# Loads, weighing and the last block of a two-layer spectral mixer: tables and odd weight copies on GpSimd's queue, one product per unit, two PSUM banks at the ends

## The chip, the cores and the metric

The kernel runs on one core of a Trainium2 chip. The metric is the device time of one execution in microseconds (us). PE is TensorE, ACT ScalarE, DVE VectorE, POOL GpSimd, SP SyncE; SP and ACT and POOL each have a queue that issues DMA transfers.

## The reference, cut to what matters

Two kinds of layers alternate, A, B, A, B, on a state x of 2048 rows by 512 columns (bf16):

```python
def _A_ref(x, w_r, w_i):          # spectral
    X = rfft2(x); X = X * (w_r + 1j * w_i)
    return irfft2(X)
def _B_ref(x, w1, w2, w3, w4):    # mixer and MLP
    h = gelu(layernorm(x) @ w1)
    # quarters of h's columns shifted by -1, +1, -2, +2 rows, then joined
    hs = concatenate([g0, g1, g2, g3]) @ w2
    x1 = x + hs
    return x1 + gelu(layernorm(x1) @ w3) @ w4
x = x + _A_ref(layernorm(x), w_r, w_i)
x = x + _B_ref(layernorm(x), ...)
x = x + _A_ref(layernorm(x), w_r, w_i)
x = x + _B_ref(layernorm(x), ...)
```

w1 and w2 are 512x512, w3 is 512x1792, w4 is 1792x512; w_r and w_i are 2048x257. Both A layers use the same weights, and so do both B layers.

## The kernel before

The state stays in SBUF as 128 partitions by 16 "rows" q of 512 columns. The code calls one A and one B together a layer, layer A in the first pass and layer B in the second (`ORDER_A`, `ORDER_B`). The Fourier transforms are products with tables: T over the partitions, FA over the columns, TL over the 16 rows q, and back through TR, G and Tinv.

A layer runs in these steps; the letter is the name of the step in the written orders.

- Norm and first product (`O`, `over_p`): the norm's factor of a row is multiplied into a copy of the table T (`Q`, `scaled_T`), PE multiplies, and the result is taken from PSUM into V (`G`, `take_V`). All 16 rows must be in V before the next step.
- `d`, `t`: product with FA for a unit of one or two blocks b of frequencies (`UNITS`: blocks 0, 1, 14, 15 are single, the rest pairs), taken into TV.
- `q`, `x`: product with TL, taken into X.
- `p` (`weigh`): X times the weights W, one product with each of the two planes, into PB.
- `b`, `m`: product with TR, taken into hT (`take_b`). Block 15 is the last; its take is divided between ACT and DVE ("B" in `TAKE_B`).
- `D`, `Y`, `P`, `a`: back over the columns and the partitions, added to x. `D` needs all 16 blocks.
- `s`, `r`, `n`, `T`, `v`, `h`, `u`, `f`: norm, DMA transpose, w1, Gelu, w2 and residual.
- `R`, `o`, `U`, `w`, `g`, `W`, `A`: norm, DMA transpose, w3, Gelu, w4 and residual. In the first pass the next layer's norm (`B`, `j`, `S`, `Q`), first products (`O`) and takes (`G`) follow between them; in the second, the stores (`y`).

TL holds two halves. The second is the first with neighbouring columns exchanged and one sign changed, made by GpSimd (`turn_TL`, L216). W is loaded for 64 of 128 partitions in 4 groups of 8 (`load_W`, L202, four copies of each group, two of them in reverse order of rows); GpSimd's queue then copies each group to the other 64 partitions (L213, called double 0 to double 3 here). Two negations (`N0`, `N1`, L710) make a third plane of TR.

What each engine does in what order is written out by hand in `ORDER_0` (the first norm), `ORDER_A` and `ORDER_B`. A step names its number, for a copy the engine (V for DVE, else ACT), and after a point the PSUM bank. `X` steps are products of zeros that keep PE at work (`fill`, L241); `z` loads the Gelu table on ACT (`gelu_table`, L712). In the first norm, rows in `ON_ACT` get their sums from ACT (`mean`, `square`, and `from_means` on GpSimd), the others theirs from DVE (bn_stats, `s`; aggregate, `i`). `S` is the square root on ACT and `J` the reciprocal on DVE; both are done once for each group of `GROUPS`.

SP issues all loads in one sequence: x, FA, half of TL, the groups of W with TR and the other half of TL between them, G and Tinv; later a small copy called gate, which reads W and so waits for double 3, and the four MLP weights behind it (`load_mlp`). The DMA transposes go through SP too. On GpSimd's queue:

```python
    for k, f in enumerate(K.later):
        if k < 2:
            turn_TL(K, slice(8 * k, 8 * k + 8))
        f()
    K.load_mlp()
```

## Time and profile before

| | us |
|---|---|
| median of 3 runs | 354.09 (353.81 to 354.54) |
| profiled execution, its own time | 354.05 |
| its span, first to last instruction | 352.1 |
| first norm ends, first `d` starts at | 21.15 |
| first `D` of layer A starts at | 42.06 |
| first `v` of layer A starts at | 57.30 |
| first `d` of layer B starts at | 189.15 |
| first `D` of layer B starts at | 208.99 |
| last matmul ends about | 348.7 |

The profile is of one execution. Times in it count from the start of the span. In a line of a timeline the first number is the start, the second the length, then the engine, the line of the source and the operation, output and input, and how many instructions were merged; in brackets how long the engine was idle before, and what ended that. A group line has the busy time, the mean length in ns, and idle time. Matmuls overlap, so that their ends are modelled. A core's DMA share is the mean over its 16 DMA engines.

### The profile page before, as it was taken

The numbers are of one execution on the slowest core, as the hardware profiler recorded it, in microseconds if no ns is written. First come the engines' busy times: TensorE is split into PE (matmuls) and PEld (weight loads), VectorE is DVE, ScalarE is ACT, GpSimd is POOL, SyncE is SP. The second block draws the span as 40 slices with busy tenths as digits, with TensorE's granted clock in tenths as the row PEclk, the third lists the DMA queues.
The fourth block names the chain that finished last, engine by engine and source line by source line (L and its number), as shares of the span: only waits on it lengthen the run. The fifth ranks groups of instructions, "written<-read, shape, count | busy, mean of one in ns | idle before, by whom it ended". The sixth has DMA issues, their size and how long they took to land.

```text
span 352.1 us, 5565 instructions
## 1 busy us (share of the span) xinstructions
PE 338.8 (96%) x2103; PEld 188.2 (53%) x2124; DVE 184.5 (52%) x442; ACT 200.5 (57%) x355; POOL 68.2 (19%) x171
## 2 busy tenths in 40 slices
PE   7889899999999999999999999999999999999996
PEld 5667785444444444444557888544444444444442
DVE  4869989669270445176586988845732004001003
ACT  5989899585736406213416979976583660442400
POOL 1430037462030101001120003645050010000000
PEclk9999999999999999999999999999999999999999
DMA  7995926611030030300000000663003005101003
GB/s 245 267 335 197 383 88 120 119 32 30 1 61 0 0 61 13 76 0 2 1 2 0 2 2 2 121 106 64 11 7 85 0 0 106 45 0 47 0 30 104
DMA packets 47210, 24.35 MB, mean 69 GB/s; under 512 B 36816, under 2 KB 43984, under 8 KB 47184
## 3 DMA queue, kind: packets, MB, share of 16 engines
q1 hardware_dynamic: 46464, 21.84, 24.7%
q0 software_dynamic: 576, 2.11, 1.5%
q8 instruction: 16, 0.26, 0.3%
q14 instruction: 10, 0.08, 0.1%
q10 hardware_dynamic: 144, 0.07, 0.1%
HBM read 11.41 MB, written 2.10 MB: 38 GB/s over the span
## 4 chain that ended last, share of the span: by engine, by line
PE 77%; ACT 8%; DMA 6%; DVE 4%; issue 3%; SPq 1%; POOL 1%; DVEq 0%; POOLq 0%; ACTq 0%
PE ps L655 26%; PE ps L642 26%; PE ps L591 8%; PE ps L607 8%; ACT hT L151 2%; PE ps L540 2%; PE ps L552 2%; DMA xT<-xn 2%; DMA W<-W 2%; PE ps L476 1%; DMA x_state<-in_A_x_dram 1%; ACT gT L649 1%; DVE PB L515 1%; ACT X L151 1%; DMA W<-in_A_w_i_dram 1%
## 5 line engine op out<-in xcount | busy, mean ns | idle before, releaser
L649 ACT ACTIVATE gT<-ps 128x1024 bf16<-128x1024 f32 x56 | 56.5, 1023 | 84.2 <-PE ps L642 81.1
L642 PE MATMUL ps<-xT,w 128*128 128x512 bf16 x448 | 99.3, 379 | 0.0
L655 PE MATMUL ps<-w,gT 128*128 128x512 bf16 x433 | 97.7, 379 | 0.8
L660 DVE TENSOR_TENSOR x_state<-ps,x_state 128x512 bf16<-128x512 f32 x32 | 21.5, 688 | 111.7 <-PE ps L655 111.7
L642 PEld LDWEIGHTS <-w 128*128 128x128 bf16 x448 | 43.8, 98 | 52.9
L655 PEld LDWEIGHTS <-gT 128*128 128x128 bf16 x448 | 43.7, 98 | 52.2
L615 DVE SCALAR_TENSOR_TENSOR xn<-xn,ln_c,ps 128x512 bf16<-128x512 bf16 x32 | 23.2, 744 | 18.5 <-PE ps L607 16.1
L270 ACT ACTIVATE junk<-xn 128x512 bf16<-128x512 bf16 x32 | 19.9, 624 | 16.8 <-DVE xn L615 16.8
L607 PE MATMUL ps<-w,hT 128*128 128x512 bf16 x122 | 28.8, 379 | 0.3
L591 PE MATMUL ps<-xT,w 128*128 128x512 bf16 x128 | 28.4, 379 | 0.5 <-DMA xT<-xn 0.5
L276 POOL TENSOR_SCALAR ln_mv<-ln_s 128x4 f32<-128x4 f32 x16 | 5.5, 344 | 91.1 <-DVE x_state L560 52.1
L560 DVE SCALAR_TENSOR_TENSOR x_state<-ps,x_state 128x512 bf16<-128x512 f32 x32 | 20.4, 684 | 2.6 <-PE ps L552 1.9
L515 DVE TENSOR_TENSOR PB<-X,W 128x1024 bf16<-128x1024 bf16 (+1 forms) x40 | 21.0, 580 | 0.1
L591 PEld LDWEIGHTS <-w 128*128 128x128 bf16 x128 | 12.3, 98 | 15.8 <-issue 1.2
L257 DVE BATCH_NORM_STATS2 ln_st<-x_state 128x6 f32<-128x512 bf16 x28 | 18.7, 686 | 3.8 <-DMA x_state<-in_A_x_dram 3.6
L607 PEld LDWEIGHTS <-hT 128*128 128x128 bf16 x128 | 12.5, 98 | 15.1
L270 ACT ACTIVATE xn<-x_state 128x512 bf16<-128x512 bf16 x32 | 19.7, 620 | 0.5 <-DVE x_state L560 0.2
L598 ACT ACTIVATE hT<-ps 128x512 bf16<-128x512 f32 x32 | 17.1, 599 | 1.4 <-PE ps L591 1.3
L540 PE MATMUL ps<-G,hT 128*128 128x256 bf16 x128 | 15.1, 273 | 2.1 <-DVE hT L149 1.2
L476 PE MATMUL ps<-FA,V 128*128 128x256 bf16 x128 | 16.1, 273 | 0.8 <-ACT V L151 0.8
L552 PE MATMUL ps<-Y,Tinv 128*128 128x256 bf16 x128 | 15.8, 272 | 0.7 <-DVE Y L149 0.5
L524 PE MATMUL ps<-TR,PB 128*128 128x128 bf16 x256 | 16.0, 219 | 0.0
(78 smaller groups left out, 387.0 us busy)
## 6 DMA issues: line engine op xcount, KB each, us to landing
w<-in_B_w_dram SPq DMA_DIRECT2D x2, 1792.0 KB, 11.9
W<-W POOLq DMA_DIRECT2D x4, 514.0 KB, 6.0
x_state<-in_A_x_dram SPq DMA_DIRECT2D x8, 256.0 KB, 5.7
out_dram<-x_state SPq DMA_DIRECT2D x16, 128.0 KB, 1.9
TR<-tab_TR SPq DMA_DIRECT2D x2, 512.0 KB, 5.8
w<-in_B_w_dram SPq DMA_DIRECT2D x2, 512.0 KB, 4.5
W<-in_A_w_r_dram SPq DMA_DIRECT2D x7, 128.5 KB, 5.7
W<-in_A_w_i_dram SPq DMA_DIRECT2D x7, 128.5 KB, 4.9
```

What stands on the lines that cost most here:

```text
L270: K.nc.scalar.activation(out, src, ACT.Square, bias=0.0, scale=D ** -0.5, accum_out=self.s[:, i, 1:2])
L515: nc.vector.tensor_tensor(t[:, :, 0:n], x, w, op=ALU.mult)
L540: nc.tensor.matmul(o[:, i, e * 256:(e + 1) * 256], lhsT=M[:, F, e, 2 * m + i, :], rhs=K.G[:, F, e, :], start=(F == 0 and e == 0), stop=(F ...
L552: nc.tensor.matmul(o[:, h * 256:(h + 1) * 256], lhsT=K.Tinv[:, c], rhs=rhs[:, ::-1] if h else rhs, start=(e == 0), stop=(e == 1))
L560: nc.vector.scalar_tensor_tensor(K.x[:, q, :], ps.pop(("P", q)), 1.0, K.x[:, q, :], op0=ALU.mult, op1=ALU.add, accum_out=ln[g].s[:, i, 0:1])
L591: nc.tensor.matmul(o[:, i], lhsT=K.w1[:, t, j * P:(j + 1) * P], rhs=xT[g][:, :, t, :], start=(t == 0), stop=(t == 3))
L607: nc.tensor.matmul(o, lhsT=K.hT[:, j, st:st + P], rhs=K.w2[:, j, :], start=(j == 0), stop=(j == 3))
L615: nc.vector.scalar_tensor_tensor(xn[:, q, :], xn[:, q, :], ln[q // 4].c[:, q % 4:q % 4 + 1], ps.pop(("u", n)), op0=ALU.mult, op1=ALU.add, ...
L642: nc.tensor.matmul(o[:, i], lhsT=K.w3[:, c, t * P:(t + 1) * P], rhs=xT3[g][:, :, c, :], start=(c == 0), stop=(c == 3))
L649: nc.scalar.activation(gT[g][:, 2 * j:2 * j + 2, :], ps.pop(("w", k)), ACT.Gelu_apprx_tanh, bias=0.0, scale=1.0)
L655: nc.tensor.matmul(o, lhsT=gT[g][:, t, i * P:(i + 1) * P], rhs=K.w4[:, t, :], start=(t == 0), stop=(t == 13))
L660: nc.vector.tensor_tensor(K.x[:, q, :], ps.pop(("W", n)), K.x[:, q, :], op=ALU.add)
```

## The change

SP loads x and then the groups of W. FA, TL and TR move to GpSimd's queue, as do the two copies of W's row 32; G and Tinv move behind the gate copy. TL's halves become contiguous. The two products of `weigh` become one of twice the size, with X read twice; PB and X get another layout for it, and the units in `LATE` share the large slots. Block 15 of the products `b`, row 15 of the first norm and row 15 of the later norm are put in two PSUM banks, one for each engine that takes them; row 15 of the first norm was taken by ACT alone before. In the first norm, two rows instead of four get their sums on ACT, groups are five instead of six, and the variance from sums is made row by row. All three orders are new; `z0` stands behind the first Gelus now, and the number of fills in the first norm falls from 16 to 12.

```diff
     for h in range(8):
         nc.sync.dma_start(K.x[:, h * 2:h * 2 + 2, :], xv[:, h * 2:h * 2 + 2, :])
-    table("FA", nc.sync)
-    K.TL = K.const.tile([P, NB, 2, P], BF16, name="TL")
+    K.W = K.const.tile([P, 2, NH, 257], BF16, name="W")
+    planes = [w.rearrange("(m j) f -> m j f", j=64) for w in (A_w_r, A_w_i)]
+    for pl, v in enumerate(planes):
+        nc.gpsimd.dma_start(K.W[2::4, pl, 0], v[:, 32])
+    for lo in range(0, NH, 8):
+        for pl, v in enumerate(planes):
+            load_W(K, v, pl, lo, lo + 8)
+    K.TL = K.const.tile([P, 2, NB, P], BF16, name="TL")
...
-        if lo == 8:
-            load_TL(slice(8, 16))
-        if lo in (0, 16):
-            nc.sync.dma_start(K.TR[:, 0:2, lo:lo + 16], dram["TR"][:, :, lo:lo + 16])
-    for k in ("G", "Tinv"):
-        table(k, nc.sync)
+
+    def load_rest():
+        q = nc.gpsimd
+        load_TL = lambda k: q.dma_start(K.TL[:, 0, 8 * k:8 * k + 8], dram["TL"][:, 8 * k:8 * k + 8])
+        load_TR = lambda k: q.dma_start(K.TR[:, 0:2, 16 * k:16 * k + 16], dram["TR"][:, :, 16 * k:16 * k + 16])
+        double = lambda k: q.dma_start(K.W[1::2, :, 8 * k:8 * k + 8], K.W[0::2, :, 8 * k:8 * k + 8])
+        table("FA", q)
+        load_TL(0)
+        load_TL(1)
+        load_TR(0)
+        double(0)
+        turn_TL(K, slice(0, 8))
+        double(1)
+        turn_TL(K, slice(8, 16))
+        double(2)
+        double(3)
+        load_TR(1)
...
         nc.sync.dma_start(gate2[:], K.W[1:2, 1, NH - 1, 1:17])
+        for k in ("G", "Tinv"):
+            table(k, nc.sync)
...
-    def from_means(self):
+    def from_means(self, i):
...
-def over_p(K, qs):
+def over_p(K, qs, split=False):
-    ps = banks(K, len(qs))
+    ps = banks(K, 2 if split else len(qs))
...
-            o = ps[:, i, t * 256:(t + 1) * 256]
+            o = ps[:, t, 0:256] if split else ps[:, i, t * 256:(t + 1) * 256]
...
     if part:
-        sl = slice(0, 64) if eng == "A" else slice(64, 128)
-    copy(K, dst[:, sl], src[:, sl], eng)
+        t = "AV".index(eng)
+        dst, ps = dst[:, 64 * t:64 * t + 64], ps[:, t:t + 1, 0:256]
+    copy(K, dst, ps.rearrange("d q (tb c) -> d tb q c", c=4), eng)
...
     def weigh(u):
         n = len(UNITS[u])
-        x = X.pop(u)[:, :, 0:256 * n].rearrange("p h (n f) -> p h n f", f=256)
-        pab[u] = []
-        for pl in range(2):
-            t = PB[n_pab[0] % 14 // 7][:, n_pab[0] % 7]
-            n_pab[0] += 1
-            w = K.W[:, pl, 2 * u:2 * u + 2 * n, 1:257].rearrange("p (n h) f -> p h n f", h=2)
-            nc.vector.tensor_tensor(t[:, :, 0:n], x, w, op=ALU.mult)
-            pab[u].append(t)
+        small = n == 1 and u not in LATE[last]
+        k = n_pab[small]
+        n_pab[small] += 1
+        if small:
+            t = PB[k % 2][:, 6].rearrange("p (l h) f -> p l h f", l=2)
+        else:
+            t = PB[k % 2][:, 2 * (k % 6 // 2):2 * (k % 6 // 2) + 2, 0:2 * n]
+        pab[u] = t
+        nc.vector.tensor_tensor(t, X.pop(u)[:, 0:2 * n].unsqueeze(1).to_broadcast([P, 2, 2 * n, 256]),
+                                K.W[:, :, 2 * u:2 * u + 2 * n, 1:257], op=ALU.mult)
...
-        ps["b", b] = o = banks(K, 1)[:, 0]
+        both = TAKE_B[last][b] == "B"
+        ps["b", b] = o = banks(K, 1 + both)
...
+        if TAKE_B[last][b] == "B":
+            F = "VA".index(eng)
+            dst, src = dst[:, :, 2 * F:2 * F + 2], ps["b", b][:, F, 0:256]
...
-FILL = {0: 4, 1: 3, 2: 3, 3: 3, 4: 3}
-GROUPS = [[0, 2, 3, 4], [7, 8, 9, 10], [11, 12], [14, 15], [1, 5], [6, 13]]
-ON_ACT = [1, 5, 6, 13]
-FIRST = [[0, 2], [3, 4], [1, 5], [7, 8], [9, 10], [11, 12], [6, 13], [14], [15]]
+FILL = {0: 3, 1: 3, 2: 2, 3: 2, 4: 2}
+GROUPS = [[0, 1, 2, 3], [4, 5, 6, 7], [8, 9, 10, 11], [12, 13], [14, 15]]
+ON_ACT = [1, 5]
+FIRST = [[0, 1], [2, 3], [4, 5], [6, 7], [8, 9], [10, 11], [12, 13], [14], [15]]
+LATE = ((14, 15), (0, 14))
 ORDER_0 = """
-s0 s2 s1 s3 i3 s5 f4 i0 i2 s4 i4 S0 s7 J0 Q0P s6 Q3V Q4V s8 s10 S4 J4 i7 O1 Q2A O0 s9 s13 Q1P i8 f5 i10 i9 Q5V s11 S1
-G1A J1 Q9V Q10V Q8P S5 s12 G0A i11 i12 O2 S2 O4 J5 Q7P s15 J2 G2A s14 i14 i15 Q12V Q11P O3 G4A Q6P S3 G3V O5 Q13A J3
-Q15V Q14P O6 G6V G5A O8 G8A O7 G7A
+s0 s2 i2 s3 i3 i0 s1 f0 s4 S0 J0 i4 Q1V Q0V s5 Q3V s6 s7 i6 i7 Q2A s11 s10 O0 G0A f1 S1 J1 s8 O1 G1A Q6A s9 Q7A i10
+i11 Q4A i9 i8 S2 s12 Q5A J2 Q10A O3 s13 G3A Q11V i13 i12 Q9V Q8V s14 S3 s15 i14 i15 O2 J3 Q12V G2A S4 J4 O5 G5A Q15A
+Q13V Q14V O4 G4V O6 G6A O7 G7V O8 G8V G8A
 """
 ORDER_A = """
...
-b14.0 m13A m11V b8.7 m8A m14V b15.5 m15A m15V D1.1 D0.5 z0 L13 Y1V Y0A D3.3 P2.0 a2 Y3A P3.7 a3 s2 P1.6 a1 P0.0 a0
...
-s13 s14 r2 P12.5 a12 L9 n8V v0.2 n11V n10V s12 r3 v1.0 h1 n9V T4 h0 v3.5 v2.0 h3 u0.7 h2 n12V n15V L14 T5 c0 u2.1 n14A
...
-S13 Q15 O15.7 A14 B14 j14 S14 Q13 O4.0 G4A G15V O6.3 G6A X4.0 Q14 O14.6 G14A X4.6 G4V G15A X8.2
...
+b13.1 m13V b8.3 m8A b14.4 m14A b15.5 m15A m15V D1.2 D0.4 D3.6 Y0A Y3A Y1V P2.1 a2 P3.4 P0.3 P1.0 s2 a3 s3 a0 s0 a1 s1
...
+n8V v0.6 v1.4 h0 c1 a14 T3 h1 T2 v3.0 s15 v2.6 s13 h3 u0.4 n10V T5 h2 u1.2 s12 f1 s14 u2.1 f2 k1 r3 c3 f0 E0 u3.7 n14V
...
+k6 w3.1 f14 E14 g3 z0 k13 L3 w1.5 g1 w4.0 g4 w0.3 g0 w2.1 g2 u9.5 f9 E6 k14 E9 E5 w6.3 E10 g6 w5.0 R1 g5 k8 E4 o4V o5V
...
+B14 O15.6 G15A S13 G4A j14 S14 Q13 O6.0 G15V G6A X4.4 Q14 O14.5 G14A X8.6 X4.5 G4V
 """
```

## The prediction

> **What bounds the kernel now.** I read the page first (busy line and chain of waits), then busy time by stage, then the timelines of single engines where a stage begins or ends. The page says that TensorE is nearly always at work:
>
> ```profile
> PE 338.8 (96%) x2103; PEld 188.2 (53%) x2124; DVE 184.5 (52%) x442; ACT 200.5 (57%) x355; POOL 68.2 (19%) x171
> ```
>
> That is an average. The stage table (stretch, length, then busy time of PE, PEld, DVE, ACT, POOL, granted clock, DMA share, GB/s) shows where it is not so:
>
> ```profile
> 3.90:21.15 17.25, 13.46 (x112) 10.75 (x110) 13.87 (x39) 15.43 (x38) 5.33 (x10) 1.00 0.96 292
> 21.15:42.06 20.91, 19.61 (x257) 15.90 (x257) 18.68 (x34) 19.13 (x27) 3.15 (x5) 1.00 0.81 298
> 42.06:57.30 15.24, 14.64 (x129) 12.43 (x130) 13.46 (x36) 14.06 (x31) 6.66 (x19) 1.00 0.53 139
> 57.30:186.00 128.70, 128.12 (x625) 60.53 (x636) 71.83 (x182) 59.24 (x102) 26.07 (x63) 1.00 0.16 30
> 189.15:208.99 19.84, 19.02 (x258) 15.95 (x256) 17.80 (x30) 17.45 (x27) 0.00 (x0) 1.00 0.01 2
> 224.00:348.70 124.70, 124.10 (x566) 56.16 (x576) 33.47 (x83) 59.10 (x101) 19.43 (x50) 1.00 0.20 42
> ```
>
> In the two long matmul stretches, 253 us, PE is busy 99.5%: nothing is won there, only lost. The change bears on the first norm (to 21.15) and on the two spectral middles (21.15 to 42.06, 189.15 to 208.99), where VectorE and ScalarE share one load at 85 to 93% each, so the sum of their work sets the length. The clock is 1.00 throughout.
>
> **Part 1, first norm.** The first product over all rows (d) starts at 21.15, when the last take of V has ended. I use the distance between starts in unbroken runs. ACT: a row's two sums 1.23 us, scaled table 0.40, pair take 0.90, square root 0.19. DVE: bn_stats 0.62, aggregate 0.09, reciprocal 0.12, scaled table 0.20, pair take 1.15. Before, ACT has 4×1.23 + 6×0.19 + 9×0.40 + 5×0.90 + 1.0 (two single takes) = 15.2; DVE 12×0.62 + 12×0.09 + 6×0.12 + 7×0.20 + 2×1.15 = 12.9. After, ACT has 2×1.23 + 5×0.19 + 7×0.40 + 6×0.90 + 0.3 (half a row) = 11.9; DVE 14×0.62 + 14×0.09 + 5×0.12 + 9×0.20 + 1.15 + 0.62 + 0.36 = 14.5. The busier engine falls by 0.7. Walking the new order by hand from the first x at 3.98, with x rows 4 and 5 at 6.46 as now, the last half take ends near 19.5: a gain of 1.65. I take 1.2, between the two.
>
> **Part 2, the loads.** SP issues x and then W alone: sixteen copies from 4.5 on by about 0.65 us end near 15, where FA, TL and TR between them made it 21.9 (two small W copies go first on GpSimd's queue, before any x has landed). FA, both halves of TL and TR now stand on GpSimd's queue behind the variances of rows 1 and 5, which it gets near 8.5. One issue there takes 0.61 to 0.87 us and landing took 6.0 to 6.6: FA at 16, needed at 19.9; TL's first half at 16.5, its turn (1.65 + 0.76) done by 19, needed by q near 21.3. Behind that turn wait double 1, the second turn, doubles 2 and 3 (which wait for W), then TR's second half. Now double 1 is held back by the second turn (GpSimd's timeline, then two pieces of the chain of waits):
>
> ```profile
> 20.18 1.65 POOL L219 TENSOR_SCALAR TL<-TL 128x512 bf16<-128x512 bf16 x1 [4.26 <-DMA TL<-tab_TL]
> 22.41 5.84 DMA W<-W
> 28.94 1.90 DVE PB L515 x3
> ```
>
> It lands at 28.25, just as DVE comes free for the products of units 2 and 4, so it costs at most 0.1. After, I expect it near 24. TR's second half, needed by its negation (N1) near 31, lands near 29. G and Tinv move behind the gate copy, which waits for double 3 (about 29); only the MLP weights stand behind them on SP; G lands near 34 and is needed near 39. I cost this part at nothing: FA is covered by 4 us, first turn and TR by about 2 each; without cover, each us late is a us lost.
>
> [...] The turn runs beside scaled tables on DVE:
>
> ```profile
> 12.79 1.66 POOL L219 TENSOR_SCALAR TL<-TL 128x512 bf16<-128x512 bf16 x1
> 12.90 0.78 DVE L348 TENSOR_SCALAR Tq<-T,ln_r 128x256 bf16<-128x256 bf16 x2
> 16.23 0.25 DVE L348 TENSOR_SCALAR Tq<-T,ln_r 128x256 bf16<-128x256 bf16 x1
> ```
>
> Two of them beside the turn took 0.78; two in a row elsewhere took 0.48: 0.3 lost. [...]
>
> **Part 3, weighing.** Two products per unit become one of twice the size:
>
> ```profile
> L515 DVE TENSOR_TENSOR PB<-X,W 128x1024 bf16<-128x1024 bf16 x24 | 15.2, 687 | 0.0
> L515 DVE TENSOR_TENSOR PB<-X,W 128x512 bf16<-128x512 bf16 x16 | 6.0, 420 | 0.1
> ```
>
> [...] One operation instead of two saves 0.07 to 0.08, ten times a layer: 0.74. The new operand reads X twice with a step of zero. No row shows that; nearest are these rows (0.53 per 1024 elements), the other end is half that rate: a pair 0.08 + 2.14 = 2.2 instead of 1.22, a single 1.15 instead of 0.69, 7.7 a layer. [...] Its free places stay as distant as now: the late units' slots are reused only after both halves of an earlier unit were multiplied. The orders also move work: in layer A one take of 128x512 (0.6) goes from ACT to DVE, so the sum of both engines falls by about 0.65, 0.3 each. In layer B the two end at about 16.6 and 17.8 against 17.8 and 17.5, so I take 0.1.
>
> **Part 4, last block in two banks.** ACT and DVE take block 15 one after the other now:
>
> ```profile
> 39.65 1.89 ACT L151 ACTIVATE hT<-ps 128x512 bf16<-128x512 f32 x4
> 41.58 0.43 DVE L149 CAST hT<-ps 128x256 bf16<-128x256 f32 x1 [0.58 <-ACT hT L151]
> 42.06 1.16 PE L540 MATMUL ps<-G,hT 128*128 128x256 bf16 x9 [1.24 <-DVE hT L149]
> ```
>
> PE stands behind both. Side by side it saves one half: 0.45 in A, 0.4 in B. The extra bank has to be free at its matmuls; it was left long before. With Part 3: 0.8 in A (0.35 + 0.45), 0.5 in B.
>
> **Part 5, turn of the layers.** DVE ends the last fold at 188.21, ACT its last take about 188.06, yet d starts at 189.15: twelve fills stand before it, four of which share the bank that ACT frees at 187.8.
>
> ```profile
> 186.23 1.83 ACT L151 ACTIVATE V<-ps 128x1024 bf16<-128x1024 f32 x3 [0.20 <-PE ps L363]
> 186.79 1.42 DVE L385 TENSOR_TENSOR V<-ps,right 128x256 bf16<-128x256 f32 x4 [0.29 <-PE ps L243]
> 187.84 1.47 PE L243 MATMUL ps<-zeros 128*128 128x256 bf16 x12 [0.68 <-ACT V L151]
> ```
>
> After, the eight (bank 6, already read) come before the four (0.11 each): d at 187.8 + 0.45 = 188.25. DVE's fold, no longer behind a fill, ends near 188. Gain 0.85.
>
> **Part 6, the Gelu table.** z0 moves behind the first Gelu, so its 1.28 us load leaves ACT's gap at 41.56 and falls before the first Gelu at 60.41, where ACT works without a gap. The new order moves four squares behind the first Gelus and has one ACT norm less (0.7). Below: 0; above: 1.28. The squares moved back make the last rows' norms later, just in time for the transposes of rows 12 to 15. I take 0.3 lost.
>
> **Sum.** 1.2 + 0.8 + 0.85 + 0.5 − 0.3 = 3.05, against the profiled execution's 354.05 (span 352.1 and 1.95 around it; the median is 354.09): 351.0. A measurement here tells about 0.2%, 0.7 us, from no change.
>
> **Rivals.** (1) The first norm gains nothing, because DVE, now the busier, is held by late x, turns or reciprocals: 1.85 remains, 352.2. For: DVE waited 0.5 for ACT's square roots twice, DMA was 96% busy. Against: rows 0 to 3 and half sums are now asked for first. (2) Slower: GpSimd's queue becomes the bound at the first products. If W goes ahead of the tables, double 0 stands behind x 2.1 MB, W 2.1, FA, TL, half TR 1.3, itself 0.5: 6.0 MB, at 292 GB/s from 1.64 it lands at 22, needed at 22.4. Each further us is lost; all 3.05 are eaten at 25.5, a rate of 250 GB/s. At 225 GB/s it lands at 28.3: 354.05 + 2.8 = 356.9. Against: the copies of 2 KB rows replace TL's of 256 B, and GpSimd's queue shares rather than waits. (3) No difference: Part 1 fails and the new order loses 1 to 2 us in the long stretches, where it can only lose: 354. (4) The product doesn't do what it says and runs at half rate: 15 us of DVE work less some 4 of slack in both middles, 362.
>
> **How the numbers follow.** Sum about right, 349.4 to 352.6: 0.62. Rival 1, 351.7 to 353.3: 0.16. Rival 3 within 0.2%: 0.07. Rival 2 and losses in the matmul stretches above 354.8: 0.12; rival 4: 0.03. So faster 0.78, same 0.07, slower 0.15. The range 349.3 to 355.0 leaves out about 0.07 below and 0.11 above.
>
> **What would show it.** d near 20, with DVE and ACT ending together; product operations of 2048 elements near 1.2 us, 20 in all; D 0.4 behind the last b in both layers; d of layer B within 0.5 of the last take of V; the table load before the first Gelu without PE idle. Idle on DVE behind DMA TR, W or FA would make it wrong, as would PE below 99% in the long stretches.

## The result, and the profile after

The changed kernel takes 350.31 us (median of 4 runs, 349.74 to 350.76), the kernel before 353.95 beside it (353.49 to 354.54): a ratio of 0.9895 with a 95% interval of 0.9874 to 0.9917, so 3.6 us faster. The forecast was 351.0 in a range of 349.3 to 355.0. The profiled execution took 350.45 with a span of 348.6, against 354.05 and 352.1 before.

The busy line of the page after says little, as before:

```profile
PE 337.2 (97%) x2100; PEld 187.9 (54%) x2120; DVE 186.2 (53%) x435; ACT 194.4 (56%) x337; POOL 73.3 (21%) x178
```

The stage table after, cut at the starts of the first `d`, the first `D` and the first `v` of each layer (columns as in the prediction: stretch, length, busy PE, PEld, DVE, ACT, POOL, clock, DMA share, GB/s):

```profile
3.90:19.56 15.66, 12.45 (x109) 10.15 (x106) 14.72 (x45) 12.84 (x27) 6.79 (x14) 1.00 0.95 307
19.56:39.70 20.14, 19.50 (x257) 16.08 (x258) 18.91 (x25) 17.92 (x25) 5.16 (x6) 1.00 0.86 298
39.70:54.54 14.84, 14.29 (x128) 12.37 (x129) 12.70 (x35) 12.84 (x30) 6.58 (x19) 1.00 0.61 169
54.54:185.78 131.24, 130.66 (x647) 62.41 (x657) 74.17 (x188) 62.98 (x106) 27.11 (x64) 1.00 0.16 30
185.78:205.63 19.85, 19.09 (x258) 16.22 (x256) 16.72 (x21) 17.91 (x26) 0.00 (x0) 1.00 0.01 2
205.63:220.32 14.69, 14.38 (x129) 12.42 (x130) 12.66 (x32) 12.58 (x29) 6.44 (x18) 1.00 0.20 38
```

The reader is to compare two rows: the middle of layer A (second) is 0.8 shorter, while the fifth row, the same middle in layer B, is as long as before (19.84), although DVE has 1.1 less work in it.

To say where time goes I use the same cuts for every kernel. The first line of the table is the kernel before, the second the changed kernel; "after, ..." is the changed kernel with one thing altered. "First D" is the start of layer A's first `D` from the start of the span; the tail runs from the start of the last residual addition on DVE to the end of the span. All are worked out from the PE and DVE timelines of one profiled execution of each.

| us | first d | middle A | first D | D to v, A | v to d | middle B | D to v, B | v to last add | tail | span |
|---|---|---|---|---|---|---|---|---|---|---|
| before | 21.15 | 20.91 | 42.06 | 15.24 | 131.85 | 19.84 | 15.03 | 124.66 | 3.42 | 352.1 |
| after | 19.56 | 20.14 | 39.70 | 14.84 | 131.24 | 19.85 | 14.69 | 124.51 | 3.77 | 348.6 |
| first norm alone | 19.68 | 22.74 | 42.42 | 15.33 | 131.85 | 19.84 | 15.28 | 124.52 | 3.46 | 352.7 |
| loads alone | 21.54 | 21.12 | 42.66 | 14.71 | 131.85 | 19.85 | 15.37 | 124.81 | 3.85 | 353.1 |
| norm and loads | 19.25 | 22.05 | 41.30 | 15.60 | 131.85 | 19.84 | 15.32 | 124.76 | 3.83 | 352.5 |
| the same, late N1 | 19.54 | 21.62 | 41.16 | 15.21 | 131.85 | 19.84 | 15.44 | 124.77 | 3.83 | 352.1 |
| after, old loads | 19.23 | 21.23 | 40.46 | 14.65 | 131.01 | 19.85 | 14.62 | 125.16 | 3.35 | 349.1 |
| after, two products | 19.96 | 20.81 | 40.77 | 14.70 | 131.35 | 20.40 | 14.66 | 124.87 | 3.75 | 350.5 |
| after, one bank | 18.81 | 20.80 | 39.61 | 14.86 | 131.23 | 20.02 | 14.69 | 124.52 | 3.87 | 348.8 |
| after, fills taken out | 18.93 | 20.44 | 39.37 | 14.73 | 130.88 | 19.86 | 14.64 | 124.52 | 3.80 | 347.8 |
| after, early table | 19.63 | 20.11 | 39.74 | 14.74 | 131.32 | 19.85 | 14.70 | 124.54 | 3.81 | 348.7 |
| after, old head of B | 19.30 | 20.14 | 39.44 | 14.75 | 131.30 | 20.30 | 14.76 | 124.52 | 3.83 | 348.9 |
| after, old tail of B | 19.23 | 20.72 | 39.95 | 15.49 | 131.01 | 19.84 | 15.32 | 124.52 | 3.77 | 349.9 |
| fills out, early V takes | 19.41 | 20.55 | 39.96 | 14.97 | 130.66 | 20.22 | 14.70 | 124.51 | 3.78 | 348.8 |

How far such a table can be read is seen in its columns. Kernels with the same first norm and loads start `d` between 18.8 and 20.0, and a later `d` mostly goes with a shorter middle A, so "first D" is the steadier measure (39.4 to 40.0 in the seven kernels that share all of the new code up to there, apart from the banks; their middle A goes from 20.11 to 20.80, so that the 0.77 of this one execution is near the upper end; what lengthens the others is told under "The turn beside the tables"). Middle B repeats within 0.02 where its order and code are the same; D to v of layer B lies at 14.62 to 14.76 with the new order and at 15.03 to 15.44 with the old.

From before to after: first `d` −1.59, middle A −0.77, D to v −0.40 and −0.34, v to `d` −0.61, middle B +0.01, then −0.15 and +0.35: −3.50 in all, the difference of the spans.

### The profile page after: what moved, and what is told of

It reads as the page before. It is cut to its first block, busy times and chain, and to the rows that moved or that the text cites. A ratio compares the mean times of both kernels' runs of the same rounds, so it can differ in the third digit from the quotient of the medians.

```text
span 348.6 us, 5541 instructions
## 1 busy us (share of the span) xinstructions
PE 337.2 (97%) x2100; PEld 187.9 (54%) x2120; DVE 186.2 (53%) x435; ACT 194.4 (56%) x337; POOL 73.3 (21%) x178
## 4 chain that ended last, share of the span: by engine, by line
PE 80%; DVE 6%; ACT 5%; issue 2%; DMA 1%; DVEq 0%
PE ps L658 28%; PE ps L671 28%; PE ps L623 8%; PE ps L607 7%; PE ps L556 3%; PE ps L568 2%; DVE PB L527 2%; PE ps L484 2%; ACT X L151 2%; ACT hT L151 1%; DMA xT<-xn 1%; DVE x_state L576 1%; ACT xn L279 1%; PE ps L508 1%; DVE hT L149 1%
## 5 line engine op out<-in xcount | busy, mean ns | idle before, releaser
L607 PE MATMUL ps<-xT,w 128*128 128x512 bf16 x128 | 28.8, 379 | 0.2
L285 POOL TENSOR_SCALAR ln_mv<-ln_s 128x4 f32<-128x4 f32 x16 | 4.6, 288 | 84.4 <-DVE x_state L576 50.1
L266 DVE BATCH_NORM_STATS2 ln_st<-x_state 128x6 f32<-128x512 bf16 x30 | 20.0, 683 | 3.9 <-DMA x_state<-in_A_x_dram 3.6
L614 ACT ACTIVATE hT<-ps 128x512 bf16<-128x512 f32 x32 | 17.9, 592 | 5.8 <-PE ps L607 5.7
L527 DVE TENSOR_TENSOR PB<-X,W 128x2048 bf16<-128x2048 bf16 (+1 forms) x20 | 19.4, 1009 | 0.4 <-ACT X L151 0.2
L302 POOL TENSOR_SCALAR ln_ve<-ln_mv 128x4 f32<-128x4 f32 (+1 forms) x15 | 4.1, 274 | 70.4 <-DVE ln_mv L295 69.7
```

The lines of the kernel that those rows point to most:

```text
L527: nc.vector.tensor_tensor(t, X.pop(u)[:, 0:2 * n].unsqueeze(1).to_broadcast([P, 2, 2 * n, 256]), K.W[:, :, 2 * u:2 * u + 2 * n, 1:257], op ...
L607: nc.tensor.matmul(o[:, i], lhsT=K.w1[:, t, j * P:(j + 1) * P], rhs=xT[g][:, :, t, :], start=(t == 0), stop=(t == 3))
```

## The experiments

"Its ratio" is that of each kernel to the kernel before, run beside it, with its 95% interval. Where a line of a written order is changed, the diff shows only the part around the change. All of the lines below stand in the profiled execution of the kernel named.

### The first norm alone

The kernel before with the new first norm: its order, groups, sums and fills, and row 15 in two banks. Nothing else is changed.

```diff
-    def from_means(self):
+    def from_means(self, i):
...
-        ps[k] = over_p(K, FIRST[k])
+        ps[k] = over_p(K, FIRST[k], k == len(FIRST) - 1)
```

> The kernel before with the new first norm alone (new groups, order of the first norm, row 15 in two banks); loads, products and layer orders as before. If the first norm's gain is its own work on ACT and DVE, the first d starts near 19.6 instead of 21.15 and nothing later gives that back: about 1.5 us faster, 352.5. Rival: the gain needed the new loads as well, since an earlier d only meets weights and turns that come as late as before (double 1 landed at 28.25, just in time): the middle of layer A then grows from 20.9 to about 22, and the kernel is less than 0.7 us faster.

353.18 us (351.73 to 354.74, 12 runs), ratio 0.9978 (0.9960 to 0.9996). The first `d` starts 1.47 earlier, but the first `D` 0.36 later. POOL's timeline, then DVE's (start, length, instruction, and in brackets the idle time before it and what ended that):

```profile
21.61 1.64 POOL L219 TENSOR_SCALAR TL<-TL 128x512 bf16<-128x512 bf16 x1 [5.58 <-DMA TL<-tab_TL]
24.12 1.28 POOL L213 DMA_DIRECT2D W<-W  x2
...
29.94 1.30 DVE L522 TENSOR_TENSOR PB<-X,W 128x1024 bf16<-128x1024 bf16 x2 [1.66 <-ACT hT L151]
```

GpSimd waits for the second half of TL, turns it, and only then issues double 1, which DVE needs for its next products. DVE, now ahead, stands for 1.66 us. The line names ACT as what ended the wait, but a wait for several semaphores is put down to the last one seen. Double 1, issued at 24.12, landed at 29.86 by the trace's record of its semaphore, and DVE went on at 29.94: it waited for double 1. Most of what the norm won is spent there. The profiled execution lies at the slow end of a wide spread, so its +0.36 is not the typical size; by the medians some 0.8 is left of 1.47.

### The loads alone

The kernel before with SP's x and W first, and FA, TL, TR, the doubles and the turns on GpSimd's queue (the first part of the diff).

```diff
-    table("FA", nc.sync)
...
+        table("FA", q)
+        load_TL(0)
+        load_TL(1)
...
-    for k, f in enumerate(K.later):
...
+    K.load_rest()
```

> The kernel before with the new loads alone: old first norm, so GpSimd gets to FA, TL and TR only behind row 5's and row 13's variances, near 12.7 instead of 8.8. If the loads as such are covered, no change, within 0.5 us of before. If GpSimd's queue can become the bound, FA lands near 18 (still covered), the first turn ends near 22.5 and the first q, at 23 before, waits up to 0.5 us; doubles 2 and 3 land 3 to 4 us later than in the full change and products wait: 1 to 3 us slower.

355.07 us (354.49 to 356.36, 12 runs), ratio 1.0035 (1.0021 to 1.0049): 1.1 us slower. In the profiled execution ACT's first sums start at 7.14 where they started at 6.46, behind x:

```profile
7.14 0.63 ACT L328 ACTIVATE junk<-x_state 128x512 bf16<-128x512 bf16 x1 [1.99 <-DMA x_state<-in_A_x_dram]
```

and FA is issued only behind the variance of the second pair of rows (POOL's timeline):

```profile
12.88 0.22 POOL L336 TENSOR_SCALAR ln_mv<-ln_mv 128x2 f32<-128x2 f32 x1
13.09 0.63 POOL L161 DMA_DIRECT2D FA<-tab_FA  x1
```

With four rows in `ON_ACT` the second pair's variance comes that late. In the new first norm there are two such rows, and FA goes at 8.85. FA still lands at 17.26, 4 us before the first `d`, so that its late issue is not what costs. Nor is it shown that the loads delay x: in the ten other kernels with the new loads x's third pair of rows lands at 5.98 to 6.77, as in the kernel before (6.44). Of the 1.0 us by which this span is longer, 0.43 is the tail, which all kernels with the new loads have; first `d` and middle A have 0.39 and 0.21. So the loads lose by themselves, under the old norm, and nearly half of the loss is at the program's end.

### First norm and loads, and the same with N1 later

Both of the edits above, still with the old orders of the layers, two products and one bank; then the same with one step moved.

```diff
-p2 p4 N1 d12.0
+p2 p4 d12.0
...
-x12A b10.7
+x12A N1 b10.7
```

> The kernel before with the new first norm and the new loads together; products, last block, fills and layer orders as before. Each alone gave 0.8 us faster and 1.1 us slower. Theory, they need each other (the norm alone was stopped at double 1, the loads alone stood behind row 5's late variance): the first d near 19.7 and the middle of layer A near 20.9, about 1.5 us faster than before, 352.4. Rival, the two simply add: 0.3 us slower than before, 354.3.

> The kernel before with the new first norm and the new loads, and in layer A's order the second negation of TR (N1) moved from behind the products of units 2 and 4 to just before the first b that needs it. In the same kernel without this move DVE stood 1.0 us before N1 for TR, which now comes last on GpSimd's queue, with takes and products queued behind it. Theory, that wait is where the norm's gain went: the middle of layer A falls from 22.1 to about 21, 353.2. Rival, the next late load (double 1, double 2) takes its place: within 0.4 us of 354.2.

354.25 us (352.83 to 356.89, 12 runs), ratio 1.0017 (0.9996 to 1.0038). The new place of TR's second half, last on GpSimd's queue, is paid for by the negation N1:

```profile
24.90 0.73 POOL L182 DMA_DIRECT2D TR<-tab_TR  x1
...
30.03 0.43 DVE L723 TENSOR_SCALAR TR<-TR 128x1024 bf16<-128x1024 bf16 x1 [0.98 <-DMA TR<-tab_TR]
```

With N1 later, 353.75 us (353.44 to 355.50, 11 runs), ratio 0.9996 (0.9985 to 1.0008): middle A is 0.43 shorter, yet the kernel is no faster than the one before. PE now stands for N1 itself, which comes too late in its new place:

```profile
33.65 1.45 PE L537 MATMUL ps<-TR,PB 128*128 128x128 bf16 x23 [0.43 <-DVE TR L723]
```

First norm and loads together put the first `D` 0.8 to 0.9 earlier, and the stretches behind it give it back: norm and loads, under the old orders, do not explain the result.

### The changed kernel with the old loads

The reverse test: everything new except the loads, which stand as before (TL's halves stay contiguous).

```diff
-    K.load_rest()
+    for k, f in enumerate(K.later):
+        if k < 2:
+            turn_TL(K, slice(8 * k, 8 * k + 8))
+        f()
```

> The full change with the loads of before (FA, TL and TR between the W copies on SP, G and Tinv behind them, turns and doubles as they were). If the loads were worth nothing in themselves, equal to the full change, 350.3 within 0.4, and the middle of layer A stays 20.1. If they are what lets an earlier d be used, double 1 lands near 26 to 28 where the new order asks for it near 26.5, and the middle of layer A grows by 0.5 to 2 us: 351 to 352.

350.81 us (349.93 to 351.63, 6 runs), ratio 0.9911 (0.9893 to 0.9929). DVE waits for a double again:

```profile
28.45 1.23 DVE L521 TENSOR_TENSOR PB<-X,W 128x2048 bf16<-128x2048 bf16 x1 [1.01 <-DMA W<-W]
```

The first `D` is 0.76 later than after, the tail 0.42 shorter; 0.65 more is lost behind the first `v` of layer B, where PE stands 0.46 for a transpose. The medians give the loads half a microsecond, the intervals overlap, and what they are worth in themselves is not shown.

### The changed kernel with two products per unit

```diff
-        nc.vector.tensor_tensor(t, X.pop(u)[:, 0:2 * n].unsqueeze(1).to_broadcast([P, 2, 2 * n, 256]),
-                                K.W[:, :, 2 * u:2 * u + 2 * n, 1:257], op=ALU.mult)
+        x = X.pop(u)[:, 0:2 * n]
+        for pl in range(2):
+            nc.vector.tensor_tensor(t[:, pl], x, K.W[:, pl, 2 * u:2 * u + 2 * n, 1:257], op=ALU.mult)
```

> The full change with two products per unit again, on the new layout. Each unit costs DVE 0.07 to 0.08 more, 0.74 per layer. Theory, DVE is the engine that sets both middles after the change (in layer B it works without a gap from its first take to D): both middles grow by 0.5 to 0.75 and the kernel is 1.0 to 1.5 us slower than the full change. Rival, the other engines set the middles and the product was hidden: less than 0.4 us slower.

351.86 us (350.80 to 352.66, 6 runs), ratio 0.9939 (0.9921 to 0.9957): 1.55 slower than after. Middle A is 0.67 longer and middle B 0.55. PE's idle before `D` is 0.87 instead of 0.50 in layer A, and it stops for 0.23 and 0.29 more within the two middles. With the new orders, each 0.74 of DVE's work is nearly all on the path.

### The changed kernel with block 15 in one bank

```diff
-        ps["b", b] = o = banks(K, 1 + both)
+        ps["b", b] = o = banks(K, 1)
...
-            dst, src = dst[:, :, 2 * F:2 * F + 2], ps["b", b][:, F, 0:256]
+            dst, src = dst[:, :, 2 * F:2 * F + 2], ps["b", b][:, 0, 256 * F:256 * F + 256]
```

> The full change with block 15's products in one PSUM bank in both layers, each engine still taking its own half. Theory: ACT and DVE take it one after the other again, D starts 0.4 us later in each layer: 0.8 us slower than the full change. Rival, D stands behind something else at that place (the last take before block 15 or the weights of D): less than 0.3 us.

351.17 us (350.40 to 355.06, 12 runs), ratio 0.9937 (0.9915 to 0.9960). DVE's half waits for ACT's, and PE for both:

```profile
39.13 0.42 DVE L149 CAST hT<-ps 128x256 bf16<-128x256 f32 x1 [0.65 <-ACT hT L151]
39.61 2.58 PE L556 MATMUL ps<-G,hT 128*128 128x256 bf16 x22 [1.17 <-DVE hT L149]
```

After, PE's idle before `D` is 0.50, so the two banks take away 0.67 of waiting in layer A; what PE does from `d` to its last product before `D` is as long in both (19.63 and 19.64). In layer B the wait is 0.68 instead of 0.51 and the middle 0.17 longer. Together that is 0.84, and the medians differ by 0.86. The spans of the two profiled executions differ by only 0.2, because this one's first `d` started 0.75 earlier (18.81 against 19.56).

### The changed kernel without the last twelve fills

```diff
-X8.6 X4.5 G4V
+G4V
```

> The full change without the twelve fills before layer B's first d (X8.6 and X4.5 taken out of the order). In the full change they run from 184.47 to 185.78 without a wait, and V is ready at 185.3. Theory, they still hold d back: d starts 0.4 to 0.5 us earlier and the kernel is that much faster, 349.9. Rival, the pause lets the granted clock drop or the first takes are not ready for an earlier d: no difference or slower.

349.58 us (348.94 to 350.42, 5 runs), ratio 0.9885 (0.9869 to 0.9901), the fastest of all. PE's timeline where layer B begins:

```profile
184.98 2.25 PE L484 MATMUL ps<-FA,V 128*128 128x256 bf16 x19 [0.69 <-ACT V L151]
```

The idle of 0.69 now ends with V itself, the granted clock is 1.00 in the window from 180 to 190 (0.998 over the execution), and v to `d` is 0.36 shorter than after. It beats both kernels by its median, by 0.7 against the changed one, though the two intervals overlap, and the ratios, each to the kernel before beside it, differ by 0.0010, which is 0.35; the stage that was edited, which otherwise lies between 131.01 and 131.35 in the kernels with the new orders, is the firmer evidence (130.66 in the other kernel without these fills).

### The Gelu table early

```diff
-g3 z0
+g3
...
-D1.2 D0.4 D3.6
+D1.2 D0.4 z0 D3.6
```

> The full change with the Gelu table's load put back into ACT's gap behind the last take of layer A's block 15 (behind D0). The prediction charged 0.3 us for its new place. If that was right, 0.3 us faster than the full change; if ACT has room before the first Gelu because four squares were moved behind it, no difference within 0.2 us; if the load delays the first Y, 0.3 to 1 us slower.

350.64 us (350.07 to 350.93, 5 runs), ratio 0.9908 (0.9895 to 0.9920); v to `d` is 131.32 against 131.24. No difference: where the load of 1.28 us stands costs nothing that these runs can tell.

### The old order of layer B's middle, then that of the rest of its spectral part

`ORDER_B` was cut at its first `D`: the old order up to there with the new one behind it (the diff below is its beginning), and the new one up to there with the old one behind it, from `D3.6 D2.0 Y2A` on.

```diff
-d15.5 t15A d4.2 t4A d1.7 d8.4 t8A t1V q1.2 x1V p1 q4.6
+d15.3 d1.6 t15A d4.0 t1V q1.2 x1A d8.4 t4V t8A q15.6 x15A p1 q4.2
...
 D3.1 D2.4 Y2A D1.6 Y1A Y3V
```

> The full change with the old order of layer B's spectral products (from its first d to its last take of b); everything else as in the full change, with the single products and the two banks. In the full change DVE gets its first take 1.95 us after d begins, in the kernel before after 1.14. Theory, DVE sets this middle, so the old order with shorter products and parallel last takes gives 1.14 + 17.5 + 0.15 = 18.8 instead of 19.85: about 1.0 us faster than the full change, 349.3. Rival, PE (19.1 busy of 19.85) or ACT sets it: less than 0.3 us faster.

> The full change with the old order of layer B from its first D to its end, behind the new spectral products. The stretch from D to the first v was 15.03 in the kernel before and 14.69 in the full change, which nothing in the prediction had. Theory, the order there makes it: the old order gives 15.0 to 15.4 again, 0.3 to 0.7 us slower than the full change. Rival, it follows from what came before (both engines free earlier at D, or the transposes' landing): the stretch stays at 14.7.

With the old head: 350.78 us (350.65 to 351.12, 4 runs), ratio 0.9908 (0.9894 to 0.9921). The theory was that the new order uses up the gain in middle B, and that the old one would give about 18.8. It fell: the old one gives 20.30. PE stops for ACT's take of X in the midst of block 15's products, DVE waits for ACT near the end, and ACT then ends the middle with six takes in a row:

```profile
201.05 3.96 PE L538 MATMUL ps<-TR,PB 128*128 128x128 bf16 x68 [0.43 <-ACT X L151]
...
203.04 0.70 DVE L527 TENSOR_TENSOR PB<-X,W 128x1024 bf16<-128x1024 bf16 x1 [0.78 <-ACT X L151]
...
202.89 2.84 ACT L151 ACTIVATE hT<-ps 128x512 bf16<-128x512 f32 x6
```

The stop of 0.43 comes from the test itself: the old order was written for one bank, and the second bank that block 15 takes there (`b15.0`, banks 0 and 1) still holds unit 6's product with TL (`q6.1`) until ACT has taken it. Moreover `b2.1` is written into that bank ahead of ACT's take of block 15 (`m15A`), so that half of block 15 is lost in this kernel; it tells a time, and is no kernel to use. Without the stop the middle would be 19.87 by this trace, as long as after: the old head is no gain either way.

With the old tail: 351.35 us (351.13 to 351.74, 5 runs), ratio 0.9921 (0.9907 to 0.9935), a microsecond slower than after; D to v of layer B is 15.32 instead of 14.69. (The spans differ by 1.3, and the other half of it lies in layer A, whose code is the same in both: PE stands 0.67 there for a transpose.) PE's last products with Tinv and the first `v`, in the kernel before, in after and in this one:

```profile
221.21 2.78 PE L552 MATMUL ps<-Y,Tinv 128*128 128x256 bf16 x24 [0.54 <-DVE Y L149]
...
217.41 2.78 PE L568 MATMUL ps<-Y,Tinv 128*128 128x256 bf16 x24 [0.19 <-ACT Y L151]
...
218.42 2.78 PE L568 MATMUL ps<-Y,Tinv 128*128 128x256 bf16 x24 [0.54 <-DVE Y L149]
221.61 0.59 PE L607 MATMUL ps<-xT,w 128*128 128x512 bf16 x2 [0.41 <-DMA xT<-xn]
```

In the new order ACT does the take that PE waits for, and 0.35 of idle goes, just what layer B's D to v lost (15.03 to 14.69). The old tail waits 0.41 more for a transpose of the first rows. So did the first norm alone, the loads alone and both, by 0.28 to 0.43, and the kernel before in its layer A, though not in its layer B:

```profile
57.30 2.96 PE L591 MATMUL ps<-xT,w 128*128 128x512 bf16 x13 [0.45 <-DMA xT<-xn]
```

After has no such wait in either layer. It is not sure to be gone: the same order of layer A has the 0.67 in the kernel with the old tail, and at most 0.17 in the other eight. What makes the transposes late was not found.

### Fills out, and DVE's takes earlier in layer B

With the old head DVE and ACT waited for each other. Here the fills are out, and DVE gets its first take one unit earlier.

```diff
-X8.6 X4.5 G4V
+G4V
...
-d15.5 t15A d4.2 t4A d1.7 d8.4 t8A t1V q1.2 x1V p1 q4.6
+d15.5 t15A d1.7 t1V d4.0 t4A q1.2 x1V p1 d8.4 t8A q4.6
```

> The full change without the twelve fills before layer B's first d (0.4 us by the run of that alone), and with the start of layer B's order changed so that DVE's first take, product with TL and take of unit 1 come before d of units 4 and 8 (unit 4's d in bank 0). Theory, DVE sets the middle of layer B and loses what it does not do at its start: its first take comes near 1.1 instead of 1.95 us after d, p of unit 4 about 0.4 earlier, and the middle falls from 19.85 to about 19.5: 349.4, against 350.3 of the full change. Rival, what DVE wins at the start it loses waiting for ACT's takes of unit 4 and 8: the middle stays 19.8 and only the fills' 0.4 remains, 349.8.

350.61 us (350.46 to 351.23, 5 runs), ratio 0.9906 (0.9889 to 0.9923). Middle B is 20.22, longer than after: PE needs 19.71 from `d` to its last product before `D`, instead of 19.34. DVE starts earlier and then stands for ACT:

```profile
186.68 0.69 DVE L149 CAST TV<-ps 128x512 bf16<-128x512 f32 x1 [1.10 <-PE ps L484]
...
190.88 1.83 DVE L527 TENSOR_TENSOR PB<-X,W 128x2048 bf16<-128x2048 bf16 x2 [1.57 <-ACT X L151]
```

## Why the prediction was right, and where it was not

The total was 0.7 too high, with the sign right and the terms for the first norm, layer A and the turn of the layers near. That the sum is so near is partly luck: the 0.5 that did not come in middle B and the 0.35 lost at the end were made up by 0.74 that no term had. Term by term, in us:

| step of the sum | predicted | measured, before to after |
|---|---|---|
| Part 1, start of `d` | −1.2 | −1.59 |
| Part 2, loads | 0 | no wait on DVE; +0.35 at the program's end |
| Parts 3 and 4, middle A | −0.8 | −0.77 |
| Parts 3 and 4, middle B | −0.5 | +0.01 |
| Part 5, turn of the layers | −0.85 | −0.84 |
| Part 6, Gelu table | +0.3 | 0, by the early table |
| D to v, both layers | 0 | −0.74 |
| rest of v to `d`; v to last add | 0 | +0.23; −0.15 |

**Part 1.** The hand walk (19.5) was nearly exact; the 0.45 between its gain of 1.65 and the 1.2 of the sum was not needed in this execution. Some of that is luck, for the walk had nothing for the turn beside the tables, where 0.7 went (below); what it had too long in turn was not looked for. But the sum treated 1.2 as won once `d` starts earlier. By itself it isn't: the first norm alone put the first `D` later. The prediction's own rows showed why, double 1 landing at 28.25 just as DVE comes free: a cover of zero, which an earlier `d` turns into a wait. Rival 1, that the first norm gains nothing, comes near for that kernel (0.8 left by the medians), though by another cause than late x or reciprocals. In the full change DVE waits for no double and no table any more; with the old orders, norm and loads did not get there, so the order of layer A, the products and the banks have their part in it. Which of them has how much was not taken apart. Rivals 2 and 3 stayed away: double 0 landed at 20.5 (22 forecast), and the long stretches did not grow (v to `d` is 0.61 shorter).

**The turn beside the tables.** The first turn fell on the tables of rows 12 to 14:

```profile
15.23 1.66 POOL L228 TENSOR_SCALAR TL<-TL 128x512 bf16<-128x512 bf16 x1 [0.87 <-DMA TL<-tab_TL]
16.83 0.83 POOL L229 COPY TL<-TL 128x512 bf16<-128x512 bf16 x1
...
16.18 0.79 DVE L358 TENSOR_SCALAR Tq<-T,ln_r 128x256 bf16<-128x256 bf16 x1
16.39 0.59 DVE L343 RECIPROCAL ln_r<-ln_r 128x2 f32<-128x2 f32 x1
16.47 1.27 DVE L358 TENSOR_SCALAR Tq<-T,ln_r 128x256 bf16<-128x256 bf16 x2
17.60 2.14 DVE L149 CAST V<-ps 128x1024 bf16<-128x1024 f32 x3
```

From 16.18 to 17.60 DVE did three tables and a reciprocal, 1.42; at the prediction's distances (0.20 and 0.12) that is 0.72. So 0.7 went, more than the 0.3 of the prediction's row. The ends tell how. The first table ends at 16.97, 0.08 behind the turn's first operation (15.23 + 1.66 = 16.89); the last ends at 17.74, 0.08 behind the second (16.83 + 0.83 = 17.66). In the kernel with the early table the turn ran sooner, and only its second operation met a table:

```profile
16.23 0.74 POOL L229 COPY TL<-TL 128x512 bf16<-128x512 bf16 x1
...
16.24 0.82 DVE L358 TENSOR_SCALAR Tq<-T,ln_r 128x256 bf16<-128x256 bf16 x1
...
17.00 0.48 DVE L358 TENSOR_SCALAR Tq<-T,ln_r 128x256 bf16<-128x256 bf16 x2
```

Again the table that met it ends 0.08 to 0.09 behind it, and the next two take their usual time. In eleven kernels sixteen tables took 0.31 to 0.91 us, and each of them ended about 0.08 behind one of the turn's operations. Those held by the first operation had begun 0.9 or more into it. Those that passed had begun within the first 0.8 us of the first operation: two before (0.58 and 0.28), three more with the old head and with one bank (0.27 to 0.29). So the prediction read its row rightly, but the two tables in that row came early in the turn; tables that came later were held, each of the sixteen to the end of one operation. Why early ones pass no run here shows.

The second turn met the negation N0 as well, in after and, longer, in the kernel with the old tail (N0 ends 0.36 and 0.27 behind that turn's first operation):

```profile
21.41 0.80 DVE L726 TENSOR_SCALAR TR<-TR 128x1024 bf16<-128x1024 bf16 x1
...
20.66 1.67 POOL L228 TENSOR_SCALAR TL<-TL 128x512 bf16<-128x512 bf16 x1
...
21.07 1.53 DVE L726 TENSOR_SCALAR TR<-TR 128x1024 bf16<-128x1024 bf16 x1
```

N0 took 0.41 where it was not held (the kernel before, the early table). It took 1.25, 1.35 and 1.53 with the fills out, with the early takes and with the old tail; right behind it PE stopped 0.15, 0.25 and 0.43 for DVE's take of X, and middle A was 20.44, 20.55 and 20.72 instead of 20.14. With the old tail N0 began only 0.4 into the operation and was held all the same, so that 0.8 is no border for every instruction. No term of the prediction had this meeting.

**Part 2.** Costed at nothing, which holds for DVE's waits: from 19.5 to 40, its list of waits (what waited, for what; us in total, times, longest) has this alone:

```profile
DVE TV L149 <- PE ps L484: 1.0, 1, 1.0
```

The dates were near: first turn done at 17.7 (19 forecast), G issued at 28.8 and landed 3.5 later (34 forecast). W's last copy was issued at 19.2 instead of 15, since SP's steady 0.65 holds only in part. TR's second half, issued at 24.50, landed at 30.15, later than the 29 forecast; it is harmless because N1 now runs at 32.91. In the old order it was a wait of 0.98. The "about 2" of cover was 2.8 under the new order and less than nothing under the old. What the sum lacks is the tail: all eleven kernels with the new loads have 3.75 to 3.87 there, and the three with the old ones 3.35 to 3.46. SP ends the program with a row of semaphore waits, one every 0.06 us. From the landing of the last store on, the kernel before has one of them left and after has eight (count, ns of one, first and last start):

```profile
L813 SPq EVENT_SEMAPHORE  x1: 28/28/28, 351.2 to 351.2; - x1
...
L830 SPq EVENT_SEMAPHORE  x8: 28/28/28, 347.3 to 347.7; - x8
```

Seven more at 0.06 are the difference: from that landing to the end of the span it is 0.92 in the three kernels and 1.34 or 1.35 in the eleven, and all of the eleven have eight waits there. The order of these waits is not written in the source; that it changed with the queues that issue the loads is seen, why is not.

**Part 3.** The product behaves as forecast; twenty in all, the pair at 1.2 us, so rival 4 falls:

```profile
L527 DVE TENSOR_TENSOR PB<-X,W 128x2048 bf16<-128x2048 bf16 x12 | 14.3, 1223 | 0.2 <-ACT X L151 0.2
L527 DVE TENSOR_TENSOR PB<-X,W 128x1024 bf16<-128x1024 bf16 x8 | 5.4, 689 | 0.2
```

That X, read twice with a step of zero, would go at the rate of the products of before was the author's estimate; no run had shown it then. After, 1024 elements more take 0.53, as there (twice 687 − 420 ns). The 0.07 to 0.08 that one operation instead of two saves shows in the timelines of before and of after too: unbroken 1024-element products start 0.60 to 0.61 apart, two in 1.21, and 2048-element products 1.13 to 1.15 apart.

```profile
28.34 2.49 DVE L515 TENSOR_TENSOR PB<-X,W 128x1024 bf16<-128x1024 bf16 x4
...
26.55 2.37 DVE L527 TENSOR_TENSOR PB<-X,W 128x2048 bf16<-128x2048 bf16 x2
```

**Part 4.** In layer A both engines end block 15 side by side, and PE's idle before `D` is 0.50 (0.4 was the mark):

```profile
37.94 1.61 DVE L149 CAST hT<-ps 128x512 bf16<-128x512 f32 x3
...
37.00 2.85 ACT L151 ACTIVATE hT<-ps 128x512 bf16<-128x512 f32 x6
...
39.70 2.78 PE L556 MATMUL ps<-G,hT 128*128 128x256 bf16 x24 [0.50 <-ACT hT L151]
```

From the first `d` to its last product before `D` PE ran 19.67 before and 19.64 after, without a stop of more than 0.1; what fell is the wait that follows, 1.24 to 0.50, and the run with one bank gives 0.67 of it to the banks. So the 0.8 came, but not for the reason that opens the prediction, that the work of DVE and ACT together sets the length of the middles: its own stage rows have PE busy for 19.61 of 20.91 and 19.02 of 19.84. As far as the modelled ends of matmuls tell, these middles are PE's unbroken work and, behind it, the last take.

**Middle B: the step that failed.** The sum took 0.1 for the products and 0.4 for the banks; nothing came. PE's waits from behind the first `d` to `D` (what waited, for what; us in total, times, longest), in before and in after:

```profile
PE ps L540 <- ACT hT L151: 0.8, 1, 0.8
...
PE ps L556 <- DVE hT L149: 0.5, 1, 0.5
PE ps L484 <- DVE X L149: 0.2, 1, 0.2
```

Before, PE works for 19.02 without a stop and then waits 0.82. After, it needs 19.34, of which 0.20 is a stop for DVE's take of X, and then waits 0.51. The last wait gave 0.31, and PE's way to it grew by 0.32. Two premises failed. The products: DVE has 1.1 less work, but PE had never waited for it before the end, so that there was nothing to shorten. The banks: block 15 is not the last in layer B's old order. Blocks 14 and 6 are taken behind it (`m15V m15A b6.5 m14V m6A D3.6`), and the 0.82 was a wait for ACT's take of block 6. Only the new order puts block 15 last, and there its two banks are worth the 0.17 of the run with one bank. As the run with two products shows, DVE can come to set this middle too, with 0.6 more work.

Seen from DVE alone, the account was another, and two experiments were built on it. DVE's first take of TV, in before and in after:

```profile
190.29 2.03 DVE L149 CAST TV<-ps 128x512 bf16<-128x512 f32 x2 [2.08 <-PE ps L476]
...
187.73 0.69 DVE L149 CAST TV<-ps 128x512 bf16<-128x512 f32 x1 [2.42 <-PE ps L484]
```

It starts 1.14 behind `d` before and 1.95 after. From there to the end of its last take DVE's stretch fell from 18.24 to 17.75, and what follows to `D` from 0.46 to 0.15, so that the 0.81 of the later start seems to use up the gain. Giving that start back (the old head, the early take) won nothing: where PE runs through, an earlier DVE has nothing to win. Which order lets PE run through and leaves the shortest last take isn't known.

**Part 5.** The gain came to a hundredth, for a reason that was only half foreseen:

```profile
183.70 1.56 ACT L151 ACTIVATE V<-ps 128x1024 bf16<-128x1024 f32 x2
...
183.90 1.41 DVE L395 TENSOR_TENSOR V<-ps,right 128x256 bf16<-128x256 f32 x4
...
184.47 1.47 PE L252 MATMUL ps<-zeros 128*128 128x256 bf16 x12
185.78 2.78 PE L484 MATMUL ps<-FA,V 128*128 128x256 bf16 x24
```

From the last first product to `d` it is 1.31 after and 2.15 before. The wait of the fills for ACT's bank is gone altogether, and all twelve run at once, not only the eight. `d` still starts 0.5 after V is complete near 185.3; taking the twelve fills out won 0.36 of that. Row 15 of the later norm in two banks stands at this place too, and was not tried by itself. What lengthened the rest of v to `d` by 0.23 was not looked for.

**Part 6 and the D-to-v stretches.** The 0.3 for the table was a loss between two bounds and should have been 0: ACT loads it at 55.06, and PE has no wait in that stretch. The −0.74 in the D-to-v stretches was not looked for, since PE is at 96% there. Both waits were in the trace of before: 0.45 for the first transpose in layer A and 0.54 for DVE's last Y in layer B. The second is shown to go with the order, by the old tail (0.54 again, 0.19 in after). The first is gone in this execution, but the wait of 0.67 in the same code shows that it need not be.

## What to carry to other kernels

An edit that makes a stage end earlier is worth only what the next stage's inputs allow: for each input list when it lands and when it will now be wanted, because a cover of zero turns every microsecond gained into a wait. Before summing what two engines save in a stretch, see whether a third runs through it without a stop: then only the wait between its last product and its next counts, and the one take that ends this wait has to be named from the written order, for each layer by itself. Parts of such a change can each be worthless or harmful alone and right together, so undo them one at a time from the full version as well as doing them one at a time from the old one.

## What the runs showed of the hardware

- DVE's product with X read twice with a step of zero took 1223 ns for 2048 elements and 689 for 1024 in after, 0.53 us for 1024 more; the products of before, with nothing read twice, took 687 ns for 1024 and 420 for 512, the same 0.53 per 1024.
- DVE's 128x256 scaled tables that met the later part of GpSimd's turn of TL (operations of 1.66 us and 0.74 to 0.84) ended about 0.08 behind the end of one of its operations, sixteen of them in eleven kernels, and took 0.31 to 0.91 instead of 0.25 to 0.29 us. Five that began within the first 0.8 us of the turn were not held to its end (0.27 to 0.58).
- In layer A of after, ACT and DVE took the two halves of block 15 side by side from two banks, and PE's wait behind the takes was 0.50 us; in the kernel with one bank it was 1.17, with DVE idle for 0.65 until ACT's take.
- A stop of PE of 0.69 us, where fills had stood, left the granted clock at 1.00 in the window from 180 to 190 around it.
- Loading the Gelu table took ACT 1.28 us, at 41.56 before, at 55.06 after and at 39.92 with the early table.
- At the end of these programs SP's waits for semaphores followed each other by 0.06 us; with eight instead of one behind the last landing the end was 0.43 longer, in eleven kernels of eleven.
